# A decode kernel that streams K, V and weights: another window at the change of layers and another last step

## The chip, the cores and the metric

The kernel runs on one core of one Trainium2 chip. The metric is the device time of one execution in microseconds. The kernel before takes 2552.23 us, the median of three runs (2552.18 to 2552.38).

## The reference

Two requests (B = 2), one new token each, pass twice through the same block: attention over a cache, and then a mixer with a wide MLP. The residual stream is x, 2 x 576. Everything is bf16.

```
def _A_ref(x, k_cache, v_cache, wq, wo):          # 32 heads, 16384 cached rows of 128
    q = (x @ wq).reshape(B, Sq, H, Dh).transpose(0, 2, 1, 3)
    scores = einsum("bhqd,bhkd->bhqk", q, k_cache) * (Dh ** -0.5)
    p = _softmax(scores, axis=-1)
    o = einsum("bhqk,bhkd->bhqd", p, v_cache)
    return o.transpose(0, 2, 1, 3).reshape(B, Sq, H * Dh) @ wo

def _B_ref(x, w1, w2, w3, w4):
    h = _gelu(_layernorm(x, axis=-1) @ w1)
    hs = (the four quarters of h, each shifted along the sequence) @ w2
    x1 = x + hs
    return x1 + _gelu(_layernorm(x1, axis=-1) @ w3) @ w4

x = A_x
x = x + _A_ref(_layernorm(x, axis=-1), A_k_cache, A_v_cache, A_wq, A_wo)
x = x + _B_ref(_layernorm(x, axis=-1), B_w1, B_w2, B_w3, B_w4)
x = x + _A_ref(_layernorm(x, axis=-1), A_k_cache, A_v_cache, A_wq, A_wo)
x = x + _B_ref(_layernorm(x, axis=-1), B_w1, B_w2, B_w3, B_w4)
```

wq is 576 x 4096, wo 4096 x 576, w3 576 x 4608 and w4 4608 x 576. The sequence is one token long, so every shift moves in zeros: the mixer's `hs` is the same in both layers and doesn't depend on x. The caches are the same in both layers too, so what stays in the chip's memory over the change of layers is not read a second time.

## The kernel before, in words

**Tiles and memory.** A pair of request and head has one K tile and one V tile, each 128 partitions x 32,768 bytes (4 MB). There are 64 such pairs, called heads 0 to 63 below. One buffer `mem` holds everything that is read: 6,144 bytes a partition at its start (`AUX`, three chunks of transposed K, `kt`) and six slots of 32,768 bytes. `Store` (L269) gives the places out.

**One queue.** All reads are planned ahead in one list (`plan_all`, L509), and go out in that order, from one queue, SP's, by one helper line (L98). A piece is issued when its place is free, that is, when the last instruction that reads what stands there has run (`release`, L322, then `pump`, L290). A later piece never overtakes an earlier one. No planner sets the order of the compute instructions; it is written out in `layer`, `attention` and `last_head`.

**A layer.** `input_norm`, then q = xn @ wq (`cols_projection`, L821; wq lies in five pieces by rows, the fifth being half as high and folded, L845), then the heads. In each head half of K is transposed on TensorE, eight blocks of 128 columns at a time, into one of four PSUM buffers `tps` (`transposed`, L1176, one "chunk"), copied back to SBUF by ScalarE (L1200), and multiplied with q on TensorE (`scores`, L1210). The other half is multiplied with q on VectorE (`dots`, L1240, L1244). Softmax follows, and P.V on TensorE (`pv`, L1300). The middle heads run in a loop of the program (`loop`). `last_head` (L1082) writes out the last head together with the start of the next projection: `shares`, `normed` and `dealt` bring the heads' outputs into the form that wo needs, and `heads_projection` (L914) runs wo piece by piece. Then `two_norms`, w3 (`cols_projection`), a gelu (`gelu_z`), and w4 (`groups_projection`, L977, with `rows_step`, L900, L908). A group of w4 is n rows of 128 in one read; `GROUPS` lists the n.

**The change of layers.** Layer 1 begins with the heads whose tiles are still there: it takes the heads in the order 63, 61, 62, 0, 1 and so on (`order`, L560). K of 61, 62, 63 and V of 62 and 63 stay (`held`, L569), in slots 1 to 5. The weights between the two layers (wo, w3, w4 of layer 0 and wq of layer 1) pass through what is left, slot 0 and `AUX`: 38,912 bytes a partition. The pieces' places are written out in `plan_all`, each over the place of an earlier one. Behind wq the list goes on with V of head 61 (slot 0, in four parts), K of head 0 (slot 1), K of head 1 in two halves (slot 3), V of head 0 (slot 4), K of head 2 (slot 5, where K of 62 was), V of head 1 (slot 0), and from there K and V in turn.

In the gaps of that stretch, chunks of K 63 are transposed ahead of time (`ahead`, L673) and copied back by ScalarE to where they came from (`lay`, L690), so that layer 1's first scores need matmuls alone (`early_scores`). The last `LEAD` = 2 chunks stay in two of the PSUM buffers until layer 1 starts (`held_over`).

**The end.** w4 of layer 1 is added into `mps` as five column tiles of 128 (the fifth begins at column 448 and overlaps the fourth). `add_rows` (L970) adds it to x in two instructions, one for the four whole tiles and one for the fifth; `finish` (L1309) transposes the five tiles back to two rows (L1316), copies them to SBUF (L1319) and writes 2 rows of 1152 bytes.

## Time and profile before

| | |
|---|---|
| median of the runs | 2552.23 us |
| the profiled execution | 2552.28 us |
| its span | 2550.6 us |
| granted TensorE clock, mean | 0.653 |
| read from HBM | 1094.21 MB, 429 GB/s over the span |
| busy: PE, VectorE (DVE), ScalarE (ACT), GpSimd (POOL) | 60%, 74%, 44%, 6% |

The span begins and ends inside the execution: 1.7 us lie outside it (2552.28 - 2550.6). The page cuts the span into 40 slices of 63.8 us; layer 0's last tile lands in the 20th, and the weights of the change of layers are read in the 20th and 21st. In a timeline row the first number is the start in us from the start of the span, the second its length; rows of the same line that follow one another are drawn together with their count, and brackets at the end name how long the engine had been idle and what it waited for. "SPq" are the issues of reads. In a row of windows come the bounds, the length, then the busy time of PE, PE's weight loads, DVE, ACT and POOL with the count of instructions, the granted clock, the busy share of the 16 DMA engines, and what they moved in GB/s. In a row of groups by line come the line, the engine, the operation, the tiles, their shapes and the count, then the busy time in us and the mean of one in ns, then the idle time ahead of them. A row of DMA issues gives the count, the size of one and the median time from issue to landing.

### The profile page before, as it was taken

To read this page: it belongs to the slowest core of one execution; us is meant where nothing else is said; L and a number is where in the kernel's file an instruction comes from. 1 tells how busy PE (TensorE), PEld (TensorE's weight loads), DVE (VectorE), ACT (ScalarE), POOL (GpSimd) and SP (SyncE) were. 2 spreads that over 40 slices of the span, in tenths; PEclk is the share of its full clock that TensorE was granted. 3 is DMA by queue.
4 is the path that set the end of the run, shared out by engine and by line. 5 is a ranking of instruction groups with operands and counts; after the bars stand their busy time and mean duration, and the time that the engine had idled before them with its cause. 6 is when DMAs were issued, how large, how long until landed. Compare 5 with 4: busy or idle time off the path is not lost.

```text
span 2550.6 us, 75213 instructions
## 1 busy us (share of the span) xinstructions
PE 1522.6 (60%) x34456; PEld 1432.9 (56%) x34456; DVE 1888.3 (74%) x1924; ACT 1113.7 (44%) x1831; POOL 162.1 (6%) x151
## 2 busy tenths in 40 slices
...
DMA  9999999999999999999999999999999999999999
GB/s 412 428 434 430 433 431 433 430 433 431 433 431 433 430 433 430 433 430 434 425 417 431 431 434 430 433 430 433 430 433 430 434 430 433 431 433 431 433 431 376
DMA packets 44900, 1094.77 MB, mean 429 GB/s; under 512 B 4922, under 2 KB 6334, under 8 KB 9662
## 3 DMA queue, kind: packets, MB, share of 16 engines
...
HBM read 1094.21 MB, written 0.00 MB: 429 GB/s over the span
## 4 chain that ended last, share of the span: by engine, by line
DMA 71%; DVE 19%; issue 8%; PE 1%; SPq 0%; POOLq 0%; DVEq 0%; ACT 0%
DMA mem<-in_A_k_cache_dram 64%; DVE s_dve L1244 9%; DVE prod L1240 9%; DMA mem<-in_A_wo_dram 3%; DMA mem<-in_B_w_dram 2%; DMA mem<-in_A_v_cache_dram 2%; DMA mem<-in_A_wq_dram 0%; DVE mx L1249 0%; PE tps L1184 0%; DVE diag L1138 0%; DVE mx L1257 0%; SPq L98 0%; DVE q_col L1129 0%; DVE o_acc L1281 0%; DVE mx L1255 0%
## 5 line engine op out<-in xcount | busy, mean ns | idle before, releaser
L1200 ACT ACTIVATE mem<-tps 128x1024 bf16<-128x1024 bf16 x1018 | 955.7, 1036 | 1290.0 <-PE tps L1184 1287.5
L1184 PE MATMUL tps<-ident,mem 128*128 128x128 bf16 x8256 | 823.3, 271 | 707.8 <-POOLq L187 707.2
L1244 DVE TENSOR_REDUCE s_dve<-prod 128x16 f32<-128x2048 bf16 x508 | 1161.3, 2286 | 17.4
L1184 PEld LDWEIGHTS tps<-ident,mem 128*128 128x128 bf16 x8256 | 677.6, 124 | 717.7 <-POOLq L187 716.8
L1240 DVE TENSOR_TENSOR prod<-mem,qb 128x2048 bf16<-128x2048 bf16 x508 | 620.6, 1222 | 527.4 <-POOLq L187 518.9
L1300 PE MATMUL mps<-p,mem 128*128 128x1 bf16 x16384 | 450.7, 165 | 85.3 <-POOLq L187 78.2
L1300 PEld LDWEIGHTS mps<-p,mem 128*128 128x128 bf16 x16384 | 443.3, 103 | 100.2 <-ACT p L1274 97.0
L1210 PE MATMUL sps<-q_col,mem 128*128 128x1 bf16 x8144 | 368.7, 167 | 159.2 <-ACT mem L1200 142.9
L1210 PEld LDWEIGHTS sps<-q_col,mem 128*128 128x128 bf16 x8144 | 320.3, 101 | 217.4 <-ACT mem L1200 212.7
L1260 POOL PARTITION_ALL_REDUCE mx<-mx x128 | 160.2, 1252 | 2331.1 <-DVE mx L1257 2331.1
L1270 ACT ACTIVATE p<-s_dve,mx 128x64 bf16<-128x64 f32 x128 | 44.5, 348 | 15.5
L1148 ACT ACTIVATE qb<-sps 128x128 bf16<-128x128 f32 x129 | 34.0, 263 | 33.5 <-PE sps L1145 33.5
L1145 PE MATMUL sps<-diag,ones_bf 128*128 128x128 bf16 x129 | 29.8, 231 | 21.6 <-DVE diag L1138 21.6
L1274 ACT ACTIVATE p<-sps,mx 128x64 bf16<-128x64 f32 x128 | 37.5, 293 | 0.0
L1268 ACT ACTIVATE mx<-mx 128x1 f32<-128x1 f32 x128 | 30.6, 239 | 14.4 <-POOL mx L1260 14.4
L1138 DVE TENSOR_SCALAR diag<-ident,q_f 128x128 bf16<-128x128 bf16 x129 | 31.6, 245 | 0.0
L1249 DVE TENSOR_REDUCE mx<-s_dve 128x1 f32<-128x64 f32 x128 | 28.2, 220 | 4.5
L835 PE MATMUL sps<-xn,mem 128*128 128x2 bf16 x544 | 21.8, 175 | 12.3 <-DMA mem<-in_A_wq_dram 6.2
L835 PEld LDWEIGHTS sps<-xn,mem 128*128 128x128 bf16 x544 | 20.7, 122 | 13.5 <-DMA mem<-in_A_wq_dram 6.8
L1255 DVE TENSOR_REDUCE mx<-sps 128x1 f32<-128x64 f32 x128 | 27.4, 214 | 0.7 <-DVEq L259 0.7
L1145 PEld LDWEIGHTS sps<-diag,ones_bf 128*128 128x128 bf16 x129 | 12.6, 97 | 22.6 <-DVE diag L1138 22.6
L1274 ACT ACTIVATION_READ_ACCUMULATOR p<-sps,mx (+1 forms) x128 | 24.2, 189 | 0.0
...
## 6 DMA issues: line engine op xcount, KB each, us to landing
mem<-in_A_v_cache_dram SPq DMA_DIRECT2D x125, 4096.0 KB, 45.5
mem<-in_A_k_cache_dram SPq DMA_DIRECT2D x124, 4096.0 KB, 43.1
...
mem<-in_A_wq_dram SPq DMA_DIRECT2D x8, 1024.0 KB, 12.5
...
```

The lines of the kernel that those rows point to most:

```text
L835: ins = pe.matmul(out[:, m * B:(m + 1) * B], lhsT=buf[:, c:c + 127 * d + 1:d], rhs=self.xn[:, k, :], start=first and m == lo, stop=False, ...
L1145: self.pe(lambda pe: pe.matmul(qps, lhsT=self.ones_bf[:, :], rhs=self.diag[:, :], start=True, stop=True, skip_group_check=True), reads=["o ...
L1148: self.act(lambda e: e.activation(out=self.qb[s % self.NS][:, :], in_=qps, func=ACT.Copy), reads=[("qps", i)], writes=[("qb", s % self.NS) ...
L1184: ins = pe.transpose(self.tps[t][:, j * 128:(j + 1) * 128], buf[:, j * 128:(j + 1) * 128], self.ident[:, :])
L1200: self.act(lambda e: e.activation(out=self.kt[k], in_=self.tps[t][:, :].rearrange("p (i c) -> p i c", i=self.CH), func=ACT.Copy), reads=[( ...
L1210: ins = pe.matmul(self.sps[sp][:, c * self.CH + j:c * self.CH + j + 1], lhsT=self.kt[k][:, j, :], rhs=self.q_col[:, sp:sp + 1], start=True ...
L1240: self.dv(lambda e: e.tensor_tensor(out=prod, in0=buf.rearrange("p (j d) -> p j d", d=128), in1=qbc, op=ALU.mult), reads=[("qb", s % self. ...
L1244: self.dv(lambda e: e.tensor_reduce(out=sd[:, c0:c0 + DB], in_=prod, axis=AX.X, op=ALU.add), reads=["prod"], writes=[("s_dve", s % self.NS ...
L1260: self.pool(lambda e: e.partition_all_reduce(self.mx[:, 3, m:m + 1], self.mx[:, 2, m:m + 1], channels=128, reduce_op=ROP.max), reads=[("mx ...
L1270: self.act(lambda e: e.activation(out=p[:, n:self.NB], in_=self.s_dve[s % self.NS][:, :], func=ACT.Exp, bias=self.mx[:, 4, m:m + 1], scale ...
L1274: self.act(lambda e: e.activation(out=p[:, 0:n], in_=self.sps[i][:, 0:n], func=ACT.Exp, bias=self.mx[:, 4, m:m + 1], scale=self.scale, acc ...
L1300: ins = pe.matmul(self.mps[:, 448:449], lhsT=buf[:, j * 128:(j + 1) * 128], rhs=p[:, col:col + 1], start=(h == 0 and b == 0), stop=(h == 1 ...
```

## The change

**What stays.** The lower half of V of head 61 (`PART`, 16,384 bytes a partition in slot 0) also stays over the change of layers; the upper half is read again in two pieces of 8,192 bytes (`REST`). `partly`, `rename` and a new count in `used` do that: places are now released in steps of 16 blocks (`UNIT`) and not by halves of a tile or whole parts.

**Where the weights pass.** The first two chunks of K 63, and not the last two, stay in two PSUM buffers, and they are put there first, at the end of layer 0's heads; the early transposes pass through the two other buffers. The place of these two chunks in slot 1 (4,096 bytes a partition) becomes part of the window. The window is then the upper half of slot 0, these 4,096 bytes and `AUX`: bytes 22,528 to 43,007 and 0 to 6,143 of `mem`, 26,624 bytes a partition. `WINDOW` lists the places of the pieces: wo in 8 pieces (before 5), w3 in 9 (7), w4 in 9 (8, by the first tuple of `GROUPS`), wq in 6 (5). K of head 0 and K of the head after it are read in four quarters each (before in one piece and in two halves).

**Order.** `last_head` calls `keep_o` ahead of `shares`, and runs the half-groups of wo in front of `normed`; `ahead` and `lay` are called at other places and other counts.

**The end.** The last layer's w4 is computed in six column tiles of 96 (`EC`); each w4 group has 128 bytes (`CELL`) of room behind it, since the last tile's weight load reads 128 columns. x is cut anew into six tiles by GpSimd copies ahead of that (`recut`), one addition takes the place of two, one transpose the place of five, and the output is written as 12 rows of 192 bytes. w1's last read is in one piece and not two.

```diff
+    def rename(self, name, new, size):
+        at, _ = self.where.pop(name)
+        for c in self.cells(at, size):
+            assert self.owner[c] == name
+            self.owner[c] = new
+        assert name not in self.owner
+        self.where[new] = at, size
...
+    UNIT = 16
     WO_CUT = 5
     PK = ["prod", "gT", "hf", "every", "y0", "y"]
-    GROUPS = (6, 6, 6, 6, 6, 3, 2, 1)
+    GROUPS = ((4, 4, 5, 5, 5, 5, 5, 2, 1), (6, 6, 6, 6, 6, 3, 2, 1))
+    WINDOW = {
+        "wo": [38400, 1536, 22528, 33792, 29184, 38400, 0, 22528],
+        "w3": [(0, 0, 33792), (0, 1, 29184), (1, 0, 24576), (1, 1, 38400), (2, 0, 1536), (2, 1, 33792), (4, None, 29184), (3, 0, 38400), (3, 1, 0)],
+        "w4": [33792, 29184, 384, 23424, 37248, 31488, 384, 37248, 39552],
+        "wq": [(1, None, 22528), (2, None, 33792), (4, None, 0), (3, None, 22528), (0, 0, 38912), (0, 1, 2048)],
+    }
+    PART = 16384
+    REST = [(24576, 8192), (16384, 8192)]
     HEAD = (200, 60)
+    EC = 96
...
         self.early = ([(h, b, 2 * pb + h * (bp - pb) + b - pb) for h in range(2) for b in range(pb, bp, ch)] +
-                      [(h, b, h * pb + b) for h in range(2) for b in range(0, pb, ch)][:-self.LEAD])
+                      [(h, b, h * pb + b) for h in range(2) for b in range(0, pb, ch)][self.LEAD:])
...
-    def plan_tile(self, T, t, u, slot, parts=1, order=None):
+    def plan_tile(self, T, t, u, slot, cuts=None):
         b, hh = u % self.B, u // self.B
         src = T[b, hh].rearrange("(p j) d -> p (j d)", p=128)
-        if parts == 1:
+        if cuts is None:
...
+        self.parts[t, u] = self.slot(slot), [lo for lo, n in cuts] + [0] * ((t, u) == self.partly())
+        for lo, n in cuts:
+            self.store.plan((t, u, lo), f"part{slot}_{lo // 4096}", self.slot(slot) + lo, n,
+                            [(lambda m: m, src[:, lo // 2:(lo + n) // 2])])
+
+    def partly(self):
+
+        return "v", self.U - self.CARRY - 1
...
-    def plan_heads(self, l, ats):
+    def plan_heads(self, l, ats, parts=1):
 
         D, hg = self.D, self.HG
-        cuts = [(i, 0, hg) for i in range(self.ng - 1)] + [(self.ng - 1, 0, self.WO_CUT), (self.ng - 1, self.WO_CUT, hg)]
+        n = hg // parts
+        cuts = [(i, j, j + n) for i in range(self.ng - 1) for j in range(0, hg, n)]
+        cuts += [(self.ng - 1, 0, self.WO_CUT), (self.ng - 1, self.WO_CUT, hg)]
...
-        for i, (n, at) in enumerate(zip(self.GROUPS, ats)):
+        for i, (n, at) in enumerate(zip(self.GROUPS[l], ats)):
             self.cuts["w4", l].append((a, a + n))
-            self.store.plan(("w4", l, i), f"w4{i}", at, 2 * n * D, [
-                (lambda m: m, self.w4[a * 128:(a + n) * 128, :].rearrange("(p j) n -> p (j n)", j=n))])
+            self.store.plan(("w4", l, i), f"w4{i}", at, 2 * n * D + gap, [
+                (lambda m, n=n: m[:, 0:n * D], self.w4[a * 128:(a + n) * 128, :].rearrange("(p j) n -> p (j n)", j=n))])
...
+        r8 = row * self.HG
         assert r8 == w3r
-        self.plan_heads(0, [a, a + r8, a + 2 * r8, 0, a + 3 * r8])
-        self.plan_cols("w3", 0, self.w3, [(0, 0, mt // 2, a), (0, mt // 2, mt, a + w3r // 2),
...
-        b = a + w3r // 2
...
-        self.plan_groups(0, [b, b + g[0], b + 2 * g[0], b + 3 * g[0], 0, g[4], b, b + g[6]])
...
-        assert e + 3 * wqr <= s[1] and wqr // 2 + wqr <= e
+
+        def halves(n, pieces):
+            return [(k, (h or 0) * n // 2, n if h != 0 else n // 2, at) for k, h, at in pieces]
+        w = self.WINDOW
+        self.plan_heads(0, w["wo"], 2)
+        self.plan_cols("w3", 0, self.w3, halves(mt, w["w3"]))
+        self.plan_groups(0, w["w4"])
+        self.plan_cols("wq", 1, self.wq, halves(hd, w["wq"]))
...
-            self.plan_tile(source[t], t, u, ring[i], (4, 1, 2)[i] if i < 3 else 1, None if i else [1, 2, 3, 0])
+            q = self.TILE // 4
+            cuts = (self.REST, [(q * j, q) for j in (1, 3, 0, 2)], [(q * j, q) for j in (0, 2, 1, 3)])[i] if i < 3 else None
+            self.plan_tile(source[t], t, u, ring[i], cuts)
...
-        self.plan_small("w1", 1, self.w1, a, (0, 56, 64))
+        self.plan_small("w1", 1, self.w1, a, (0, 64))
...
-            if self.made == len(self.early):
-                if len(self.held_over) < self.LEAD:
-                    c = 2 * self.PB // self.CH - self.LEAD + len(self.held_over)
-                    self.transposes(1, 0, self.order(1)[0], c)
...
-            h, b, col = self.early[self.made]
-            self.made += 1
-            self.laid.append((h * self.BP + b, self.chunk % self.NT))
-            self.transposed(self.order(1)[0], h * self.BP + b)
+            u = self.order(1)[0]
+            c = len(self.held_over)
+            if c < self.LEAD:
+                at = self.chunk + len(self.early) + c
+                self.held_over.append((0, u, c, at))
+                self.transposed(u, c * self.CH, ("t", c), at % self.NT)
+                self.used(1, "k", u, c * self.CH, self.CH)
+            elif self.made < len(self.early):
+                h, b, col = self.early[self.made]
+                t = self.made % (self.NT - self.LEAD)
+                assert all(x != t for _, x in self.laid)
+                self.made += 1
+                self.laid.append((h * self.BP + b, t))
+                self.transposed(u, h * self.BP + b, None, t)
...
+        self.ahead(1 - l, 1)
...
-        self.ahead(l, 3)
+        self.ahead(l, 2)
...
-        self.lay(l, 4)
+        self.lay(l, 3)
...
+        if l == self.NL - 1:
+            self.recut()
+
+    def recut(self):
...
+        at = [(t, p) for t in range(KT) for p in range(0 if t < KT - 1 else TL, 128, 32)]
...
+            self.pool(lambda e, t=t, p=p, j=j, q=q, n=n: e.tensor_copy(out=self.x6[q:q + 32 * n, j, :],
+                                                                      in_=self.x[p:p + 32 * n, t, :]),
+                      reads=["x"], writes=["x6"])
+            g += n
...
-                        at = [self.block_cols(w, m + h * n // 2) for h in range(2)]
+                        at = [self.block_cols(w, m + h * n // 2, l) for h in range(2)]
...
                         for i, (c, d) in enumerate(at[:1] if at[0] == at[1] else at):
...
+    def rows_step(self, buf, a, b, ps, rhs, rk, pk, nm, first, m=128):
...
+        cols = self.kcol if m == 128 else range(0, D, m)
...
-                    o = (k - a) * D + self.kcol[t]
+                for t, c in enumerate(cols):
+                    o = (k - a) * D + c
...
             self.rows_step(self.store.buf(nm), a, b, self.mps, lambda k: self.gT[:, k * self.B:(k + 1) * self.B],
-                           "gT", "mps", nm, i == 0)
-            if i < 3:
+                           "gT", "mps", nm, i == 0, 128 if l < self.NL - 1 else self.EC)
+            if i < 3 or i == 4:
                 self.ahead(l, 1)
-            if i < 4:
+            if i < 6:
                 self.lay(l, 1)
             if i == 1:
                 self.side_norm(l)
             if i == 2 and l == self.NL - 1:
                 self.h_projection()
-        last = l == self.NL - 1
-        self.add_rows(self.xo[:, :, :] if last else self.x, "xo" if last else "x", self.mps, "mps")
+        if l < self.NL - 1:
+            self.add_rows(self.x, "x", self.mps, "mps")
+            return
+        m = self.EC
+        self.tt(self.xo[0:m, :, :].rearrange("p b t -> p t b"), self.x6[0:m, :, :],
+                self.mps[0:m, 0:self.ET * self.B].rearrange("p (t b) -> p t b", b=self.B), ALU.add,
+                ["x6", "mps"], ["xo"])
...
-        self.ahead(l, 1)
+        self.lay(l, 1)
+        self.ahead(l, 2)
         self.softmax_exp(s)
         self.touch(ACT.Sqrt)
         self.lay(l, 2)
         self.landed("v", u, False)
         for g in range(4):
             self.pv(l, s, u, g)
+        self.keep_o(s, None)
+        n = [sum(c[0] < a for c in self.cuts["wo", l]) for a in (1, 2)] + [len(self.cuts["wo", l])]
+        for i in range(n[0]):
+            self.heads_projection(l, i)
         self.shares(first, U)
-        self.keep_o(s, None)
-        self.heads_projection(l, 0)
         self.normed(l, first, U)
+        for i in range(n[0], n[1]):
+            self.heads_projection(l, i)
         self.dealt(late, U, self.sps[0], ("sps", 0), self.masked[1], self.oB[:, :], "oB")
-        self.heads_projection(l, 1)
         self.ahead(l, 1)
         self.lay(l, 1)
-        for i in range(2, len(self.cuts["wo", l])):
+        for i in range(n[1], n[2]):
             self.heads_projection(l, i)
...
-        parts = 2 if whole else self.parts[t, u]
-        size = self.NB // parts
-        part = b0 // size
-        self.uses[t, u, part] = self.uses.get((t, u, part), 0) + n
-        if self.uses[t, u, part] == size:
+        size = self.UNIT
+        for part in range(b0 // size, (b0 + n - 1) // size + 1):
+            k = min(b0 + n, (part + 1) * size) - max(b0, part * size)
+            self.uses[t, u, part] = self.uses.get((t, u, part), 0) + k
+            if self.uses[t, u, part] < size:
+                continue
             del self.uses[t, u, part]
+            lo, step = part * size * 256, size * 256
             if whole:
-                self.store.release((t, u), part * self.TILE // 2, (part + 1) * self.TILE // 2)
+                if l == 0 and (t, u) == self.partly() and lo < self.PART:
+                    continue
+                self.store.release((t, u), lo, lo + step)
             else:
-                self.store.release((t, u, part))
-
-    def transposed(self, u, b0, sig=None):
+                at = max(x for x in self.parts[t, u][1] if x <= lo)
+                self.store.release((t, u, at), lo - at, lo - at + step)
+        if l == 0 and whole and (t, u) == self.partly() and b0 + n == self.NB:
+            self.store.rename((t, u), (t, u, 0), self.PART)
...
+    def transposed(self, u, b0, sig=None, t=None):
...
-        self.chunk += sig is None
+        t = self.chunk % self.NT if t is None else t
...
-        def f(pe):
-            for t in [KT - 1] + list(range(KT - 1)):
-                c = self.kcol[t]
-                ins = pe.transpose(mb[0:B, c:c + 128], self.xo[:, t, :], self.ident[:, :])
-            return ins
-        self.pe(f, reads=["xo", "ident"], writes=["mps"])
-        self.dv(lambda e: e.tensor_copy(out=self.rows[0:B, 0:D], in_=mb[0:B, 0:D]), reads=["mps"], writes=["prod"])
-        o = g.dma("out", [(self.out.rearrange("b s d -> (b s) d"), self.rows[0:B, 0:D])], reads=["prod"])
+        m, n = self.EC, self.ET * B
+        self.pe(lambda pe: pe.transpose(mb[0:n, 0:m], self.xo[0:m, :, :].rearrange("p b t -> p (b t)"),
+                                        self.ident[0:m, 0:m]), reads=["xo", "ident"], writes=["mps"])
+        rows = self.rows[0:n, 0:m]
+        self.dv(lambda e: e.tensor_copy(out=rows, in_=mb[0:n, 0:m]), reads=["mps"], writes=["prod"])
+        o = g.dma("out", [(self.out.rearrange("b s (t c) -> (b s t) c", c=m), rows)], reads=["prod"])
```

74 lines of the change are left out of this document (32 added, 42 removed).

## The prediction

> **What bounds the kernel now.** I read the page first (totals, slices, queues, chain), then the windows and the DMA view of the plateau and of the change of layers, and last the timeline of the change and of the end.
>
> ```profile
> span 2550.6 us, 75213 instructions
> ...
> PE 1522.6 (60%) x34456; PEld 1432.9 (56%) x34456; DVE 1888.3 (74%) x1924; ACT 1113.7 (44%) x1831; POOL 162.1 (6%) x151
> ...
> DMA  9999999999999999999999999999999999999999
> GB/s 412 428 434 430 433 431 433 430 433 431 433 431 433 430 433 430 433 430 434 425 417 431 431 434 430 433 430 433 430 433 430 434 430 433 431 433 431 433 431 376
> ...
> HBM read 1094.21 MB, written 0.00 MB: 429 GB/s over the span
> ```
>
> All 40 slices have the DMA engines at nine tenths or more, and no compute engine is busy for more than 74% of the span. The kernel is a read of 1094 MB; it is faster only if it reads less, or loses less where the rate drops: slices 19 and 20 (change of layers) and the last.
>
> ```profile
> 1262.00:1275.00 13.00, 10.23 (x308) 9.77 (x308) 1.34 (x7) 2.62 (x3) 0.00 (x0) 0.50 1.01 417
> 1275.00:1288.00 13.00, 11.25 (x200) 11.01 (x201) 2.98 (x24) 4.86 (x8) 0.00 (x0) 0.50 1.01 411
> 1288.00:1300.00 12.00, 9.46 (x212) 8.30 (x209) 1.85 (x12) 5.51 (x7) 0.00 (x0) 0.50 1.02 418
> 1300.00:1312.00 12.00, 8.56 (x185) 7.97 (x186) 1.89 (x13) 3.51 (x5) 0.00 (x0) 0.50 1.02 424
> ```
>
> The last two numbers of a row are DMA share and GB/s. During the change of layers the queue is never empty (share 1.0), although the rate is 411 to 424 and not the 430 to 434 of most slices. So today's window for the weights hides every chain of small operations, and what is lost there is the price of small rows:
>
> ```profile
> DMA packets 8900, 259.08 MB, mean 432 GB/s; under 512 B 992, under 2 KB 992, under 8 KB 992
> ...
> DMA packets 1582, 9.11 MB, mean 414 GB/s; under 512 B 176, under 2 KB 176, under 8 KB 1021
> ...
> q8 instruction: 3, 0.05, 0.9%
> ```
>
> The first row is 400 to 1000 us, the others 1262 to 1284. Two equations, time = bytes/rate + packets x c/16, give c = 11.4 ns a packet on each engine. The last row: three packets of instructions took 0.9% of 16 x 22 us, 1.06 us each, on one engine each.
>
> **Part 1, bytes.** Half of V tile 61 is not read again: 2.10 MB at 432 GB/s is -4.85 us, if the queue stays full (-5.0 at the 418 of this stretch).
>
> **Part 2, more pieces.** wo is read in 8 pieces instead of 5, w3 in 9 for 7, w4 in 9 for 8, wq in 6 for 5; the rest of V 61 in 2 for 4, the first K tile of layer 1 in 4 for 1, the second in 4 for 2. That is 12 more; a piece is 128 rows and 16 semaphore writes, so 12 x 144 / 16 x 11.4 ns = +1.2 us while the queue is full, and nothing where it waits for an issue anyway. With the gaps found below I take a third, +0.4 (0 to 1.2).
>
> **Part 3, the smaller window.** Before, weights pass through 38,912 B a partition, 4.98 MB or 11.9 us at 418 GB/s. After, 16,384 + 6,144 + 4,096 = 26,624 B: 3.41 MB, 8.2 us. A freed place costs a round trip (issue, first data, last of 16 semaphore writes), which a deep queue hides. Its price from the only tile that meets an idle queue:
>
> ```profile
> 0.79 0.39 SPq L98 DMA_DIRECT2D mem<-in_A_k_cache_dram  x1
> ...
> mem<-in_A_k_cache_dram SPq DMA_DIRECT2D x1, 4096.0 KB, 12.5
> ```
>
> 12.5 us less 4.194 MB / 432 GB/s = 9.7 leaves 2.8 us fixed. Lower bound: the 2.2 KB of output are issued at 2549.01 and the span ends at 2550.6, so 1.6. Upper: one instruction packet in the way, 2.8 + 1.06 = 3.9. I take 2.8, because it is a load, through all 16 engines, as the pieces are.
>
> The Trainium skill, "DMA: Bandwidth & Descriptors" (section "Anatomy of one DMA"), puts the fixed cost at about 2.0 us, fitted on the path through GpSimd; this trace's 2.8 is above it. With 2.0 the sum would be 2549.6 (rival a) instead of 2553.5.
>
> The other durations, from the timeline of the change (PE, DVE, SP):
>
> ```profile
> 1225.69 0.33 SPq L98 DMA_DIRECT2D mem<-in_A_v_cache_dram  x1
> ...
> mem<-in_A_v_cache_dram SPq DMA_DIRECT2D x1, 4096.0 KB, 36.9
> ```
> ```profile
> 1257.15 1.04 PE L932 MATMUL sps<-l,mean_f 128*128 128x48 f32 x4
> ...
> 1262.80 3.55 PE L1300 MATMUL mps<-p,mem 128*128 128x1 bf16 x128 [1.55 <-POOLq L187]
> ...
> 1267.07 1.21 PE L908 MATMUL sps<-oA,mem 128*128 128x2 bf16 x40
> ...
> 1268.31 22.54 SPq L98 DMA_DIRECT2D mem<-in_B_w_dram  x15
> ...
> 1274.01 0.56 PE L908 MATMUL sps<-oB,mem 128*128 128x2 bf16 x15
> ...
> 1275.76 2.74 PE L1184 MATMUL tps<-ident,mem 128*128 128x128 bf16 x24
> ...
> 1278.37 3.25 PE L835 MATMUL sps<-xn,mem 128*128 128x2 bf16 x72
> ...
> 1284.15 1.14 PE L845 MATMUL sps<-xt,mem 128*128 128x4 bf16 x24
> ...
> 1286.78 0.89 PE L835 MATMUL sps<-xn,mem 128*128 128x2 bf16 x18 [0.40 <-DMA mem<-in_B_w_dram]
> ...
> 1289.05 0.96 PE L908 MATMUL mps<-prod,mem 128*128 128x2 bf16 x30 [0.50 <-DVE prod L1000]
> ...
> 1299.12 0.65 PE L908 MATMUL mps<-prod,mem 128*128 128x2 bf16 x15 [0.18 <-DMA mem<-in_B_w_dram]
> ...
> 1302.61 0.99 PE L835 MATMUL sps<-xn,mem 128*128 128x2 bf16 x32
> ...
> 1310.55 1.02 PE L835 MATMUL sps<-xn,mem 128*128 128x2 bf16 x32 [1.83 <-DMA mem<-in_A_wq_dram]
> ...
> 1316.03 1.23 DVE L1240 TENSOR_TENSOR prod<-mem,qb 128x2048 bf16<-128x2048 bf16 x1 [1.47 <-PE sps L1210]
> ...
> 1330.84 1.22 DVE L1240 TENSOR_TENSOR prod<-mem,qb 128x2048 bf16<-128x2048 bf16 x1
> ...
> 1345.81 0.33 SPq L98 DMA_DIRECT2D mem<-in_A_k_cache_dram  x1
> ```
>
> I walk the ring with two rules. A piece lands bytes/418 GB/s after the one before it, but not before its issue + 2.8 + bytes/418; it is issued 0.1 us after the last matmul that reads what stood in its place, in order (above, matmuls that end at 1267.07 + 1.21 = 1268.28 and an issue at 1268.31). 4,608 B a partition take 1.41 us, 5,760 take 1.76, 8,192 take 2.5, 4,096 take 1.25. On the kernel before, these rules give the end of the wq matmuls at 1311.6, as the row has it (1310.55 + 1.02). V 63 lands at 1225.69 + 36.9 = 1262.6 in both. After the change:
>
> wo: the first piece waits for the two chunks of K 63 to pass to PSUM and for the PE operation that then runs, 1257.15 + 1.04, about 1258.3; the queue still holds V 63, so nothing is lost. Pieces land 1264.0 to 1269.7. The P.V product ends at 1266.3, and two half-heads (0.61 each) free a place at 1266.9; that piece lands at 1271.2, the last at 1274.0; matmuls end 1274.6, as before (1274.57). The fixed 2.8 first shows here, by 0.1.
>
> w3: two pieces are in flight; the third place is freed by the last of wo (1274.6), so it lands at 1278.9 instead of 1278.2. PE starts 3.6 us after wo (now 3.8: 1274.57 to 1278.37, three chunks of transposes of 0.91 stand before it, later two). A half-piece takes 0.9 (0.89 by its row); the fourth freed place is issued at 1279.1; the tail piece needs 36 matmuls for 24, as the halves of the uneven groups no longer pair (1.7 for the row's 1.14). w3 ends at 1288.4 (before 1287.7).
>
> w4: gelu 1.4 us; pieces land at 1289.0, 1290.8, 1293.1 (its place is freed at 1288.4), then 1.8 apart to 1300.2, 1301.0, 1301.4. End 1301.6 (before 1299.8).
>
> wq: the second piece waits for the last of w4, 1301.7, and lands at 1307.0; the fourth waits for the first, which PE starts 2.8 after w4; the halves land at 1312.1 and 1313.7. End 1314.2 (before 1311.6): +2.6.
>
> The gaps of these four stages add to 3.1 us. Of V 61 and the two K tiles nearly nothing waits. Then layer 1 computes two heads from tiles already there, bound by DVE, so K of head 2, the sixth of the order, issued at 1345.81 into the place of the second of those heads when that is done, now goes out at 1348.4. V of head 0, before it, has landed at 1348.9: a last gap of 2.3 us. K lands at 1361.2, against 1345.81 + 15.2 = 1361.0:
>
> ```profile
> mem<-in_A_k_cache_dram SPq DMA_DIRECT2D x1, 4096.0 KB, 15.2
> ```
>
> After that a head takes 14.8 us of DVE (1316.03 to 1330.84) and two tiles, 19.4 us, of DMA, so DMA is the bound again and everything shifts alike. So parts 1 and 3 together are 5.5 us of gaps against 5.0 saved, +0.5. To it I add instruction packets: about eight of 1.06 us fall between 1259 and 1312, a piece is there when the slowest engine has it, and a deep queue hides that where a shallow one does not: 0 to 8 us, I take 1.0, near the low end, as most fall on an engine that is ahead. The other new waits cost nothing here: with two PSUM buffers instead of four for the early transposes, a transpose waits for the ScalarE copy two back, 1.04 us each and done a stage earlier; if that cover goes, it is 1 us each on PE, four times at most.
>
> ```profile
> L1200 ACT ACTIVATE mem<-tps 128x1024 bf16<-128x1024 bf16 x1018 | 955.7, 1036 | 1290.0 <-PE tps L1184 1287.5
> ...
> L1316 PE MATMUL mps<-ident,xo 128*2 128x128 bf16 x5 | 0.7, 302 | 0.5 <-DVE xo L596 0.5
> ```
>
> (The groups by line; the second row is for the end.) SP's queue holds nothing but these loads, so behind a piece that waits stand only later pieces.
>
> **Part 4, the end.**
>
> ```profile
> 2546.70 0.66 PE L908 MATMUL mps<-prod,mem 128*128 128x2 bf16 x15 [0.17 <-DMA mem<-in_B_w_dram]
> 2547.39 0.36 DVE L596 TENSOR_TENSOR xo<-st,mps 128x8 bf16<-128x8 f32 x2 [3.00 <-PE mps L908]
> 2547.80 0.69 PE L1316 MATMUL mps<-ident,xo 128*2 128x128 bf16 x5 [0.45 <-DVE xo L596]
> 2548.54 0.45 DVE L1319 COPY prod<-mps 2x576 bf16<-2x576 bf16 x1 [0.79 <-PE mps L1316]
> 2549.01 0.27 SPq L98 DMA_DIRECT2D out_dram<-prod  x1
> ```
>
> After the last piece 18 matmuls for 15 (+0.13), one addition for two (-0.18), one transpose for five (0.30, row L1316, for 0.69: -0.39), a copy of 12 x 96 for 2 x 576 (0.22 for 0.45, an estimate: the additions of 8 columns take 0.18 each: -0.23): -0.65, between -1.0 and +0.5. The extra matmuls before and the GpSimd copies of x lie under the DMA, which PE waits for. The Trainium skill, same page, "Specifications", says that transfers under 512 B are read, modified and written; the output rows fall from 1152 to 192 B, and no run here prices that.
>
> **Sum.** 2552.28 (profiled run, 0.05 above the median 2552.23) + 0.5 + 0.4 + 1.0 - 0.65 = 2553.5 us.
>
> **The rivals.** (a) The window is deep enough: with the output's round trip of 1.6 the same walk ends wq at 1311.1. Then only K of head 2, still issued at 1345.8 because compute got no faster, leaves a gap, of 1.1; K and V land 3.9 us earlier; with part 2 in full and part 4, 2552.28 - 3.9 + 1.2 - 0.65 = 2548.9. A round trip 0.4 longer ends wq at 1311.3 and gives 2549.6, the other end of this case. For it: share 1.0 in every window now, and the output's 1.6. Against: 2.8 at the first tile. The Trainium skill's 2.0 (the section above) would be this case. (b) The other side, slower: the round trip is 3.5 to 3.9, since the slowest of 16 engines meets an instruction packet on most turns. At 3.5 the walk ends wq at 1318.4 and the V tile after K at +5.4, which with parts 2 and 4 is 2557.4; at 3.9, +8.4 and 2560.4. So 3.5 is where it passes 0.2%. For it: 1.06 us each, one every 7 us, against seven turns that depend on each other; against: now no wait shows them. (c) The tail does not get shorter, since small output rows cost what the copies save: +0.65 on any case.
>
> **How the numbers follow.** Forecast case 2550 to 2557: 0.52. (a) 0.24. (b) 0.24. Can't be told from no change within 0.2%, 5.1 us, 2547.1 to 2557.3. Even full hiding, with no gap at all, gives 2552.28 - 4.85 + 1.2 - 0.65 = 2548.0, so faster by more than 0.2% is 0.04; slower is nearly all of (b), 0.22; same 0.74. The range leaves out a tenth at each end: 2548.2 to 2560.
>
> **What would show it.** Right: bytes read 2.1 MB fewer; weights landing 4 to 6 us after issue instead of 7 to 11; DMA share under 1 in some windows from 1265 to 1350, most near 1348; wq ending near 1314; the last addition to the output's issue about 1.0 us instead of 1.6. Wrong: share 1.0 throughout and K of head 2 issued at 1345.8 (a); wq after 1318 (b).

## The result: slower by 9 us, and the profile after

The changed kernel takes 2561.33 us, the median of six runs (2560.58 to 2564.74); the kernel before takes 2552.20 beside it (2551.95 to 2552.38). The ratio is 1.0038, with a 95% interval of 1.0025 to 1.0051: +9.1 us, where 2553.5 was forecast. The profiled execution is the fastest of the six, 2560.58 us.

The page after, totals and slices:

```profile
span 2558.7 us, 75319 instructions
...
DMA  9999999999999999999999999999999999999999
GB/s 409 430 432 431 433 431 431 434 429 432 434 430 431 433 431 431 433 431 431 409 349 423 432 433 430 432 432 431 433 431 431 433 431 432 431 432 433 430 432 380
...
HBM read 1092.11 MB, written 0.00 MB: 427 GB/s over the span
```

The 2.10 MB are saved. The plateau is as before. The whole loss is in slices 20 to 22: 409, 349 and 423 GB/s, where before had 425, 417 and 431. The windows of that stretch (bounds, length, busy time of PE, weight loads, DVE, ACT and POOL with counts, granted clock, DMA share, GB/s), after:

```profile
1262.00:1275.00 13.00, 10.97 (x315) 10.24 (x313) 1.47 (x7) 3.98 (x5) 0.00 (x0) 0.50 0.99 384
1275.00:1288.00 13.00, 8.72 (x169) 8.11 (x170) 3.20 (x25) 3.72 (x6) 0.00 (x0) 0.50 0.96 355
1288.00:1300.00 12.00, 8.72 (x172) 7.65 (x170) 1.72 (x11) 5.85 (x8) 0.00 (x0) 0.50 0.95 349
1300.00:1312.00 12.00, 7.33 (x154) 6.29 (x152) 1.69 (x11) 4.53 (x6) 0.00 (x0) 0.50 0.86 322
1312.00:1324.00 12.00, 6.79 (x203) 6.38 (x201) 1.19 (x7) 2.75 (x5) 0.00 (x0) 0.50 0.95 333
```

Look at the last two numbers together. The share still says 0.95 while the rate is 349: a packet that is under way counts as busy however slowly it goes, so in this stretch only GB/s tells how much is lost. The trace keeps every packet, and a data packet here is one partition's row of a piece: of the 4,229 data rows that begin in 1262 to 1324, 164 took more than twice the median of their size (the longest 2.33 us, where the median is 0.31); before, it was 19 of 3,704. Over 1262 to 1324 after moved 21.53 MB and before 25.94; the 4.41 MB between them are 10.5 us at 418 GB/s. Two more views, the DMA issues of 1268.2 to 1291 us (count, size, median us from issue to landing) and the timeline of PE, show the same from the side of the pieces:

```profile
mem<-in_B_w_dram SPq DMA_DIRECT2D x11, 576.0 KB, 5.6
```
```profile
1273.45 1.44 PE L956 MATMUL sps<-oB,mem 128*128 128x2 bf16 x40 [1.17 <-DMA mem<-in_A_wo_dram]
...
1289.17 0.84 PE L882 MATMUL sps<-xn,mem 128*128 128x2 bf16 x18 [0.55 <-DMA mem<-in_B_w_dram]
...
1306.06 0.29 PE L956 MATMUL mps<-prod,mem 128*128 128x2 bf16 x5 [1.42 <-DMA mem<-in_B_w_dram]
...
1317.93 1.01 PE L882 MATMUL sps<-xn,mem 128*128 128x2 bf16 x32 [3.96 <-DMA mem<-in_A_wq_dram]
...
1320.45 0.58 PE L882 MATMUL sps<-xn,mem 128*128 128x2 bf16 x16 [0.70 <-DMA mem<-in_A_wq_dram]
```

The eleven pieces of 4,608 bytes a partition in that view (nine of w3, two of w4) land 5.6 us after their issue by the median; the forecast's price of a place is 2.8 + 1.41 = 4.2. PE ends wo at 1274.89, w3 at 1290.01, w4 at 1306.35 and wq at 1321.03 (start plus length of the rows), against 1274.6, 1288.4, 1301.6 and 1314.2 by the walk. The wait of 3.96 us is for a wq piece whose place came free late (issue at 1310.07), but not for that alone. A read is shared by the 16 DMA engines, and the trace has 16 landing signals for each: 15 parts of this piece were there by 1315.34, and the last at 1317.89.

K of head 2 then goes out, in the timeline of SP, and its DMA row gives the time to landing:

```profile
1355.35 0.33 SPq L98 DMA_DIRECT2D mem<-in_A_k_cache_dram  x1
...
mem<-in_A_k_cache_dram SPq DMA_DIRECT2D x1, 4096.0 KB, 15.7
```

The table follows the landings, after minus before:

| piece | before | after | shift | gap added here |
|---|---|---|---|---|
| end of w3 | 1286.74 | 1289.12 | +2.4 | 2.2 (V 63 was at +0.2) |
| end of w4 | 1299.43 | 1306.02 | +6.6 | 4.2 |
| end of wq | 1310.51 | 1320.40 | +9.9 | 3.3 |
| K of head 1 | 1341.39 | 1349.54 | +8.1 | 3.1 (with 4.85 saved at V 61) |
| K of head 2 | 1361.00 | 1371.07 | +10.1 | 1.9 |
| last weight piece | 2547.01 | 2555.85 | +8.8 | |
| output's issue | 2549.01 | 2557.07 | +8.1 | |

The gaps add to 14.7 us; the forecast had 5.5. About 1.0 us comes back between the last V tile (+9.8) and the last weight piece.

The end, in the timeline after:

```profile
2553.60 2.62 PE L956 MATMUL mps<-prod,mem 128*128 128x2 bf16 x72 [0.95 <-DMA mem<-in_B_w_dram]
2556.32 0.19 DVE L619 TENSOR_TENSOR xo<-x,mps 96x12 bf16<-96x12 f32 x1 [3.04 <-PE mps L956]
...
2556.57 0.24 PE L1375 MATMUL mps<-ident,xo 96*12 96x96 bf16 x1 [0.35 <-DVE xo L619]
2556.85 0.20 DVE L1378 COPY prod<-mps 12x96 bf16<-12x96 bf16 x1 [0.34 <-PE mps L1375]
2557.07 0.34 SPq L98 DMA_DIRECT2D out_dram<-prod  x1
```

From the end of the last matmul (2556.22) to the output's issue it is 0.85 us, before 1.65. This part does what it says.

### The profile page after: what moved, and what is told of

It reads as the page before. It is cut to its first block, busy times and chain, and to the rows that moved or that the text cites. A ratio compares the mean times of both kernels' runs of the same rounds, so it can differ in the third digit from the quotient of the medians.

```text
span 2558.7 us, 75319 instructions
## 1 busy us (share of the span) xinstructions
PE 1526.8 (60%) x34500; PEld 1438.4 (56%) x34500; DVE 1888.2 (74%) x1923; ACT 1114.5 (44%) x1831; POOL 164.4 (6%) x163
## 4 chain that ended last, share of the span: by engine, by line
DMA 70%; DVE 20%; issue 8%; PE 1%; SPq 1%; POOLq 0%; DVEq 0%; ACT 0%
DMA mem<-in_A_k_cache_dram 64%; DVE s_dve L1305 9%; DVE prod L1301 9%; DMA mem<-in_B_w_dram 3%; DMA mem<-in_A_wo_dram 2%; DMA mem<-in_A_v_cache_dram 1%; SPq L98 0%; DMA mem<-in_A_wq_dram 0%; DVE mx L1310 0%; DVE diag L1195 0%; DVE mx L1318 0%; DVE q_col L1186 0%; DVE o_acc L1342 0%; DVE mx L1316 0%; PE tps L1245 0%
## 5 line engine op out<-in xcount | busy, mean ns | idle before, releaser
L1342 DVE COPY o_acc<-mps 128x1 f32 (+1 forms) x130 | 19.3, 149 | 7.6 <-PE mps L1361 7.6
```

## The experiments

The theory behind the forecast: a freed place costs a constant round trip, and the window holds enough pieces to hide nearly all of it. The result is 9 us off that, so the runs ask three things: is it the window or another part of the change; does the round trip of a place stay constant; do instruction packets make it long (the reason that rival (b) gave)?

### One part alone: the end

`before` with the six tiles of 96, `recut` and the one transpose, and with nothing of the change of layers; and the same with w1's last read in one piece.

```diff
+    EC = 96
...
-        self.plan_groups(1, [b, s[1], ...])
+        self.plan_groups(1, [b, s[1], ...], CELL)
...
+        if l == self.NL - 1:
+            self.recut()
```


> The kernel before with the new end alone (six column tiles, one addition, one transpose, 12 rows of output). The prediction's sum for it is -0.65 us, 2551.55 against 2552.2; the trace of the changed kernel has 1.22 us from the last landing to the output's issue where the kernel before has 2.00, so -0.8, 2551.4. The rival that small output rows cost what the copies save: 2552.2.

```diff
-        self.plan_small("w1", 1, self.w1, a, (0, 56, 64))
+        self.plan_small("w1", 1, self.w1, a, (0, 64))
```


> As e1_tail, and w1's last read in one piece of 64 rows and not 56 + 8. The prediction gave that edit nothing: then 2551.4 as e1_tail. The trace of the changed kernel has w1 there 0.35 us before the last piece of wo, where before it came 1.24 us behind it; if that is worth something at the end, it is 0.65 us: 2550.8.

The end alone takes 2551.51 us (2551.29 to 2551.90) against 2552.24 beside it: -0.73; the ratio is 0.9997 (0.9988 to 1.0006), so the interval alone doesn't tell it from none, but the slowest of its 11 runs is only 0.04 above the fastest of the 33 of before (2551.86). With w1's cut it is 2551.78 (2551.66 to 2552.12), so that cut costs 0.27 and gains nothing. The forecast's -0.65 for the end holds, and the loss lies in the change of layers.

### The window, with everything else kept

The changed kernel with the whole of V 61 read again, so that the window is 43,008 bytes, and the same pieces at other places; 28 to 32 KB a partition of reads stand behind each piece as far as the end of w4, then 15 to 22 KB for wq.

```diff
-    PART = 16384
-    REST = [(24576, 8192), (16384, 8192)]
+    PART = 0
+    REST = [(8192, 8192), (16384, 8192), (24576, 8192), (0, 8192)]
...
-        "wo": [38400, 1536, 22528, 33792, 29184, 38400, 0, 22528],
+        "wo": [6144, 10752, 15360, 22528, 27136, 31744, 0, 38912],
```


> The changed kernel with all its small pieces, but V 61 is not kept: its lower half's place joins the window (43,008 bytes a partition), and each piece has its place where 28 to 32 KB were read behind the piece that stood there. V 61 is read whole again, 2.1 MB or 4.85 us more. Theory (small window, round trip longer than 2.8 us): no gaps, 2552.2 + 0.4 to 1.2 for pieces - 0.65 to 1.4 for the end = 2551 to 2553. Rival (the pieces and their packets cost it): the loss stays and the bytes come on top, 2561.3 + 4.9 = 2566; anything above 2558 speaks for it.

The second keeps a quarter of V 61, with a window of 34,816 bytes.

```diff
-    PART = 16384
+    PART = 8192
```


> As the changed kernel, but a quarter of V 61 is kept and not a half: window of 34,816 bytes a partition, 23 KB read behind most pieces before their place is needed (the changed kernel: 14 KB; at 418 GB/s 7.1 and 4.2 us). Theory (small window): a place is needed again later than a round trip of 4.1 us plus the piece's 1.4, so gaps only at wq (0 to 3 us): 2552.2 - 2.4 - 0.65 to 1.4 + 0.4 to 1.2 + 0 to 3 = 2548 to 2553. Rival (pieces): about 2563.7.

The first takes 2555.03 us (2554.09 to 2557.25; ratio 1.0013, interval 1.0004 to 1.0022), which is 6.3 us faster than the changed kernel although it reads 4.85 us more, and still 2 us above the 2551 to 2553 that were expected. Its windows (columns as above):

```profile
1275.00:1288.00 13.00, 9.51 (x193) 8.95 (x194) 3.28 (x25) 3.72 (x6) 0.00 (x0) 0.50 1.02 410
...
1300.00:1312.00 12.00, 7.93 (x169) 6.79 (x166) 1.70 (x11) 4.54 (x6) 0.00 (x0) 0.50 0.92 352
```

Up to the end of w4 it is late by 0.72 us, of which 0.22 is V 63: six more pieces cost 0.5, where the forecast's 144 / 16 x 11.4 ns a piece gives 0.6. So the new order, the two PSUM buffers and the many pieces cost next to nothing there. What it loses it loses behind w4, +1.55 at wq and +2.6 at V 61: at the very places where I had left only 15 to 22 KB. The changed kernel, with 9 to 18 KB, has 14.7 us of gaps to this one's 3.7 (K of head 2 lands 3.92 late, less 0.22). The smaller window is what costs the 11 us between them.

The quarter takes 2555.05 (2553.66 to 2557.09; ratio 1.0009, interval 1.0000 to 1.0018), also above what was expected (2548 to 2553). Its wq pieces had only 9 to 12 KB behind them, and its wq ends 4.98 us late.

### A round trip by itself

All layers are left out; what is computed is no longer the reference. 72 pieces of 4,608 bytes a partition (590 KB, 1.41 us at 418 GB/s) pass through n = 1 to 6 places, 12 for each n; 18 matmuls read a piece and free its place.

```diff
+        for depth in (1, 2, 3, 4, 5, 6):
+            for i in range(12):
+                nm = ("piece", depth, i)
+                a = (len(todo) % 7) * n // 2
+                self.store.plan(nm, f"piece{i % depth}", self.slot(0) + (i % depth) * n, n, [(lambda m: m, flat[:, a:a + n // 2])])
...
+        for nm in todo:
...
+                for c in range(18):
...
+            self.store.release(nm)
```


> The round trip by itself, with nothing else running: pieces of 128 x 4,608 bytes of K pass through 1, 2, 3, 4, 5 and then 6 places (12 pieces each), each piece read by 18 matmuls and its place given to the next. All layers are left out, so its output and its time are not the kernel's. If the fixed part of a round trip is the forecast's 2.8 us, one place gives a period of 0.1 + 2.8 + 1.4 + about 0.9 = 5.2 us, and four places keep the queue full (period 1.4). If it is the 4.1 us that makes the forecast's walk end where the changed kernel did, one place gives 6.5 us and four do not.

The windows of the ring, one stretch for each n from 1 to 6 (bounds, length, PE, weight loads, POOL, granted clock, DMA share, GB/s), and below them the DMA issues in the same stretches (count, size, median us from issue to landing):

```profile
9.00:53.00 44.00, 6.39 (x180) 5.58 (x180) 0.00 (x0) 1.00 0.45 134
60.00:87.00 27.00, 6.41 (x180) 5.59 (x180) 0.00 (x0) 1.00 0.73 218
92.00:111.00 19.00, 5.75 (x162) 5.01 (x162) 0.00 (x0) 1.00 0.84 281
115.00:133.00 18.00, 5.82 (x165) 5.02 (x162) 0.00 (x0) 1.00 0.98 334
137.00:152.00 15.00, 5.76 (x162) 5.02 (x162) 0.00 (x0) 1.00 1.00 373
162.00:173.00 11.00, 4.47 (x126) 3.90 (x126) 0.00 (x0) 1.00 1.02 402
```
```profile
mem<-in_A_k_cache_dram SPq DMA_DIRECT2D x10, 576.0 KB, 3.7
...
mem<-in_A_k_cache_dram SPq DMA_DIRECT2D x10, 576.0 KB, 4.8
...
mem<-in_A_k_cache_dram SPq DMA_DIRECT2D x9, 576.0 KB, 5.2
...
mem<-in_A_k_cache_dram SPq DMA_DIRECT2D x11, 576.0 KB, 6.0
...
mem<-in_A_k_cache_dram SPq DMA_DIRECT2D x8, 576.0 KB, 6.8
...
mem<-in_A_k_cache_dram SPq DMA_DIRECT2D x5, 576.0 KB, 7.8
```

One piece alone takes 3.7 us, which leaves 2.3 of fixed cost: less than the forecast's 2.8. But the time grows with the pieces in flight, and does so before the rate is full: by the forecast's rules one to four places give about 120, 240, 360 and the full 418 GB/s, and these windows have 134, 218, 281 and 334. Five and six places, 23 and 28 KB a partition, give 373 and 402. The share reads 0.98 at 334 GB/s, much as in the changed kernel. A window also holds the pieces with which one depth passes into the next, and instruction packets; for four places and more that makes it low, as the next run shows.

The Trainium skill, "DMA: Bandwidth & Descriptors" (section "Anatomy of one DMA"), has about 2.0 us that scale with nothing, for a DMA issued from GpSimd (these are issued from SP). For one piece alone the 2.3 here is near it; two in flight take 4.8 us, 3.4 past a piece's own bytes, so no one constant describes a place.

### The same with fewer instructions, and in other cuts

Two matmuls instead of 18 for a piece, so that the whole run reads one instruction packet and not ten, and none in the stretches below (and PE is 0.5 us quicker with a piece); layers left out as above.

```diff
-                for c in range(18):
+                for c in (0, 17):
```


> The ring of e5 (1 to 6 places of 4,608 bytes, 12 pieces each, layers left out), but 2 matmuls read a piece and not 18, so that there is hardly an instruction packet (one for e5's nine). Theory that these packets make the stalls of e5's rings of 3 to 6 places: with F = 2.3 a piece takes 2.3 + 1.4 + 0.2 = 3.9 us round, so three places already run at a period of 1.4 us without a stall. Rival (a piece that reaches the engines when they are about to run dry starts anew, whatever the packets): two places keep e5's period of 2.75 and not 1.95, and three still stall.

The windows for n = 2, 3 and 4:

```profile
52.00:75.00 23.00, 2.13 (x20) 1.31 (x20) 0.00 (x0) 1.00 0.82 253
80.00:98.00 18.00, 1.91 (x18) 1.18 (x18) 0.00 (x0) 1.00 0.91 303
103.00:118.00 15.00, 1.92 (x18) 1.18 (x18) 0.00 (x0) 1.00 0.99 365
```

For one to six places it is 151, 253, 303, 365, 402 and 411 GB/s. With two, a piece comes every 2.33 us (0.590 MB / 253 GB/s), where the 2.3 of a lone piece would give 1.95, and three do not fill the engines either: there, instruction packets are not the reason. Four is another matter. Landing by landing, the pieces of this run with four places in use come 1.46 us apart from 109.79 to 120.00, which is 404 GB/s; the next comes 2.48 us later, and the run's one packet of 16 KB begins at 119.15. In the first ring they come 1.39 to 1.42 us apart from 121.06 to 135.84, but for one gap of 3.55, beside a packet at 127.14. So four places run nearly full where no packet meets them, and a packet of 0.9 to 1.0 us on one engine comes with a loss of 1.1 and of 2.1 us.

What two and three places lack is to be seen in the landing signals and the rows of this run, counted for each n from its n-th landing to its last:

| places | issue to first of 16 parts, median us | first to last part, median us | rows over twice the median (0.18 us) | GB/s |
|---|---|---|---|---|
| 1 | 3.2 | 0.5 | 180 of 1408 | 148 |
| 2 | 3.3 | 1.2 | 148 of 1292 | 247 |
| 3 | 3.4 | 1.7 | 71 of 1087 | 326 |
| 4 | 4.2 | 2.1 | 25 of 1039 | 372 |
| 5 | 5.2 | 1.6 | 7 of 761 | 417 |
| 6 | 6.1 | 2.2 | 0 of 606 | 416 |

With one to three places the first part lands 3.2 to 3.4 us after the issue: the start gets hardly dearer. It is the last part, the one that frees the place, that falls further behind. Of a lone piece the first 16 rows, which begin 0.95 to 1.60 us after its issue, take up to 1.04 us, and nearly all later ones about 0.18; with one and two places there are about 16 slow rows for each piece (180 for 11 pieces, 148 for 10), with five and six hardly any. The reading that fits is that an engine which has run dry begins anew with a slow row, and that a piece waits for the slowest of 16. Which engine moved a row is not in the trace, and why such a row is slow stays open.

Then 18,432 bytes as 2, 4 and 8 pieces, and 27,648 bytes as 3, 6 and 12.

```diff
+        for k, (n, depth, pieces) in enumerate([(9216, 2, 12), (4608, 4, 24), (2304, 8, 48), (9216, 3, 12), (4608, 6, 24), (2304, 12, 48)]):
```


> The same 18,432 bytes of places cut as 2 x 9,216, 4 x 4,608 and 8 x 2,304, then 27,648 bytes as 3, 6 and 12 (layers left out; every 128 x 128 block read by one matmul). If the bytes in flight alone count, the rate is one and the same for a size of the ring: about 320 GB/s for the first three (e5 with four places: 316) and about 400 for the others. If a finer cut helps, since a place is given back sooner, 8 places are nearer to full rate than 2; with 2 places of 9,216 the formula 2.3 + 2.8 + 1.3 = 6.4 us for 2 pieces gives 369 GB/s.

The windows in that order:

```profile
5.00:40.00 35.00, 11.95 (x389) 11.16 (x390) 0.00 (x0) 1.00 0.94 350
45.00:78.00 33.00, 13.12 (x373) 11.40 (x370) 0.00 (x0) 1.00 0.99 367
84.00:116.00 32.00, 16.23 (x369) 12.87 (x366) 0.00 (x0) 1.00 1.04 389
122.00:150.00 28.00, 10.30 (x332) 9.57 (x333) 0.00 (x0) 1.00 1.00 409
...
190.00:222.00 32.00, 17.07 (x393) 13.63 (x390) 0.00 (x0) 1.00 1.06 391
```

It is mostly the bytes in flight that count: 18 KB a partition give 350 to 389, 27 KB give 391 to 411. Finer pieces help a little where bytes are few (350 to 389), and cost where they are enough (409 to 391). With eight places of 2,304 bytes the pieces come 0.75 us apart nearly throughout, where 418 GB/s would be 0.71: that ring hardly runs dry, and what it lacks is the price of shorter rows.

### Finer pieces in the kernel

If that holds in the kernel, finer cuts of wo, w3, w4 and wq through the same 26,624 bytes should gain. Two forms; the first lays two pieces into the first 6,144 bytes of `mem`.

```diff
-    GROUPS = ((4, 4, 5, 5, 5, 5, 5, 2, 1), (6, 6, 6, 6, 6, 3, 2, 1))
+    GROUPS = ((2, 2, 2, 3) * 3 + (3, 2, 2, 2), (6, 6, 6, 6, 6, 3, 2, 1))
...
-        self.plan_heads(0, w["wo"], 2)
+        self.plan_heads(0, w["wo"], 4)
```


> The changed kernel with the same window (half of V 61 kept) and its weights cut about half as large (wo 14 pieces, w3 17, w4 16, wq 9): about 18 KB are then read behind a piece before its place is needed, where the changed kernel has 9 to 18. If the ring's table holds in the kernel (18,432 bytes as 4 pieces 371 GB/s, as 8 pieces 389; 13,824 bytes as 3 places 293), w3, w4 and wq go from the 322 to 355 GB/s of the changed kernel's windows to 370 to 390: 15.3 MB, 44 us before and 39 to 41 after, so -3 to -5 us, 2556.5 to 2558. If more pieces only cost packets (24 more, 2.5 us by the 11.4 ns of the prediction): 2564.

> e11 cut its weights finer and lost 16 us, but its trace shows matmuls of wo that waited 6.6 us for the landing of a w3 piece beside theirs: two pieces shared a 2,048-byte unit of the first 6,144 bytes, by which the kernel keeps its waits. Here one piece at a time stands there, and 13 to 18 KB are read behind a piece (changed kernel: 9 to 18). By the ring (8 pieces of 2,304: 389 GB/s, 4 of 4,608: 352 to 371, 3: 293): -2 to -4 us, 2557 to 2559.5. If finer pieces only cost packets: 2563 or more.

The first takes 2577.71 us (2577.27 to 2578.44), 16 more than the changed kernel, and by a fault of its own, which the timeline of PE shows:

```profile
1279.43 1.23 PE L956 MATMUL sps<-oA,mem 128*128 128x2 bf16 x40 [6.57 <-DMA mem<-in_B_w_dram]
```

A wo matmul waits 6.57 us for a w3 piece: the program keeps waits by cells of 2,048 bytes, the two pieces (2,304 bytes each) share one, and so the earlier one's reader waits for the later one too. It says nothing of the theory. The second form has no shared cell and takes 2564.52 (2564.05 to 2566.24; ratio 1.0049, 1.0035 to 1.0062): 3 us more than the changed kernel, where 2 to 4 less were expected. The number is that of the expectation's other case (finer pieces only cost packets, 2563 or more), but the windows do not show a full queue with dearer rows. With 13 to 18 KB behind a piece of wo and w3 (in the changed kernel 9 to 18) this stretch ran slower than there (332 GB/s for 355), and in 1262 to 1324 there are 226 slow rows for 164:

```profile
1275.00:1288.00 13.00, 7.07 (x148) 6.06 (x144) 3.27 (x25) 3.72 (x6) 0.00 (x0) 0.50 0.94 332
```

The expectation of a gain falls. Why finer pieces help in the ring and not here stays open.

### A quarter, with deeper places for wq

The quarter again, with wq in halves and places with 15 to 32 KB behind each.

```diff
-        "wq": [(1, None, 34816), (2, None, 21376), (4, None, 30592), (3, None, 34816), (0, 0, 0), (0, 1, 14336)],
+        "wq": [(1, 0, 512), (1, 1, 26624), (2, 0, 30720), (2, 1, 34816), (4, None, 38912), (3, 0, 14336), (3, 1, 18432), (0, 0, 512), (0, 1, 22528)],
```


> e4 (a quarter kept, 34,816 bytes) with wq in halves and places such that 15 to 32 KB are read behind every piece, where e4 had 9 to 12 at wq. Theory: no gap up to V 61; then K of head 2 is issued at about 1345.9 as in the kernel before, since compute sets it, so that of the 2.4 us of bytes only what is left at its landing counts (e8: 0.3 of 1.2): 2552.25 - 0.75 for the end - 0.3 + 0.5 to 1.2 for pieces = 2551.5 to 2552.5. Rival (the bytes come through in full): 2550.

It takes 2553.69 us (2552.99 to 2554.96), 1.4 less than the first quarter, at 1.0006 of before (0.9997 to 1.0015). The end of wq is 2.87 us late and not 4.98 (the first quarter's profile is of its slowest run, so about 2 us of its lateness are that run's). Placing alone moves the time, but a window of 34,816 bytes still costs more than the quarter saves: with the shorter end in it the kernel stands 1.5 us above before (2552.20), which the interval does not tell from none, and above the 2551.5 to 2552.5 that were expected.

### Instruction packets

896 one-column memsets on GpSimd in the middle of `last_head`, in the kernel before and in the changed one: they work on a tile of their own, and only make GpSimd read more instructions.

```diff
+        if l == 0:
+            def f(e):
+                for c in range(32):
+                    ins = e.memset(self.idle[:, c:c + 1], 0)
+                return ins
+            for _ in range(28):
+                self.pool(f, writes=["idle"])
```


> The kernel before, and 896 tiny GpSimd instructions (writes of one byte a partition to a place nobody reads) behind the landing of V 63, which bring 3 to 4 more instruction packets of 16 KB into the change of layers. No gaps there, so every theory expects 0 to +1 us (the packets' bytes are 0.15 us; one engine falls 1 us behind at a time).

> The same 896 GpSimd instructions in the changed kernel. Theory that instruction packets set what a round trip takes above 2.8 us (the queue runs dry, all engines wait for the one that was late): 3 to 4 packets x up to 1 us, +2 to +4 us, 2563 to 2565. Rival (the round trip is longer by itself): 0 to +1, 2561 to 2562.

Both came out against the theory. The changed kernel takes 2561.21 us (2560.86 to 2562.17), as without them, where 2 to 4 us more were expected. The packets that came were seven of 8 KB and 0.3 to 0.5 us, though, not the 3 to 4 of 16 KB that the expectations speak of. The kernel before takes 2555.18 (2554.41 to 2556.16; ratio 1.0012, 1.0003 to 1.0021): +2.9, where a deep queue was to hide them. Its DMA view of 1262 to 1324 has seven packets more than before's one:

```profile
q14 instruction: 8, 0.07, 0.3%
```

They come about every 4.85 us, and the last of a piece's landings falls behind its first by steps of 0.65 to 0.75 us at that pace, to 5.65 us (before 2.9). The signals show how: of the fifth w4 piece 15 parts are there by 1297.29 and the last at 1300.26, where before has 1297.12 and 1297.29. So one of 16 parts falls behind by some 3 us, and while the queue is full it does not catch up. That it is the engine which carries these packets is argued from the pace and not shown. VectorE is slower beside the memsets too (4.53 us busy for 2.98 in 1275 to 1288), but compute is not what delays this stretch: 15 parts of the last w4 piece land only 0.16 us later than before. In the changed kernel with the packets the last part stays within 1.1 us of the fifteenth up to the end of wq; its queue runs dry between pieces, which would let such an engine catch up, and that is argued, too.

### The rule used for a better version

An eighth of V 61 is kept (4,096 bytes), in return for the 4,096 bytes of the two chunks in PSUM: the window stays at 38,912 bytes, with the kernel before's larger pieces. The order, the PSUM buffers and the end are those of the change.

```diff
-    GROUPS = ((4, 4, 5, 5, 5, 5, 5, 2, 1), (6, 6, 6, 6, 6, 3, 2, 1))
+    GROUPS = ((6, 6, 6, 6, 5, 4, 2, 1), (6, 6, 6, 6, 6, 3, 2, 1))
...
-    PART = 16384
-    REST = [(24576, 8192), (16384, 8192)]
+    PART = 4096
+    REST = [(12288, 8192), (20480, 8192), (28672, 4096), (4096, 8192)]
```


> The changed kernel with an eighth of V 61 kept (4,096 bytes a partition) and not a half: the two chunks of K 63 in PSUM give back just what the eighth takes, so the window is 38,912 bytes as before, and the pieces are those of before (one w4 group apart). Theory (the loss is all in the small window): no gaps, 2552.24 - 1.05 MB / 432 GB/s (2.4... a quarter would be; the eighth is 0.52 MB, 1.2 us) - 0.7 for the end = 2550.3, within 0.5. Rival (something else in the change costs: the two PSUM buffers, the order in the last head): 2551.5 or more.

It takes 2551.23 us (2550.71 to 2552.29) against 2552.26 beside it: -1.03, where -1.9 was expected; ratio 0.9997, interval 0.9988 to 1.0006. It is the fastest kernel of the study, by a difference that the interval does not tell from none. Its windows are full again, and K of head 2 goes out where it did before:

```profile
1275.00:1288.00 13.00, 10.75 (x200) 10.32 (x201) 3.23 (x25) 3.95 (x7) 0.00 (x0) 0.50 1.01 409
...
1300.00:1312.00 12.00, 7.92 (x173) 6.92 (x174) 1.74 (x13) 4.54 (x6) 0.00 (x0) 0.50 1.02 420
```
```profile
1345.91 0.33 SPq L98 DMA_DIRECT2D mem<-in_A_k_cache_dram  x1
...
mem<-in_A_k_cache_dram SPq DMA_DIRECT2D x1, 4096.0 KB, 14.8
```

w4 lands at -0.03 and wq at +0.12 to before, so the two PSUM buffers and the new order cost nothing. V 61 lands 0.99 early, V of head 0 still 0.68, K of head 2 only 0.32: it is issued at 1345.91 (before 1345.81), when the compute of the first heads has freed its place, and no byte saved ahead of it brings that forward. Nearly all of the gain is the end's.

## Why the prediction was wrong

**Part 1, bytes: right in size, without effect.** 2.10 MB less are read, and V 61 alone recovers 4.85 us of the shift. But K of head 2 waits for compute, and compute for wq: wq ends 9.46 us late (1321.03 for 1311.57), K goes out 9.54 late (1355.35 for 1345.81) and lands 10.1 late. The saved bytes stand between the two and are used up by the wait. The forecast had this step ("now goes out at 1348.4", a last gap of 2.3), and the eighth of V 61 shows the same on an undisturbed window.

**Part 2, more pieces: right.** 0.5 us for six more pieces with a full queue; 0.4 was taken for twelve with gaps.

**Part 3, the smaller window: the step that failed is "I take 2.8", one fixed price for every freed place.** By it four pieces of 4,608 bytes fill the queue, and the gaps come to 5.5 us. Measured are 14.7. The start of a piece is not dearer than forecast (a lone piece takes 2.3 past its bytes), but a place comes free only when the last of 16 parts is in, and with two and three pieces in flight this comes 1.2 to 1.8 us behind the first, where a lone piece has 0.5. So two and three places gave 218 and 281 GB/s in the ring, where 2.8 gives about 240 and 360. The changed kernel, which leaves 9 to 18 KB behind a piece, so two to four pieces, ran at 322 to 384. There, too, the first part landed as early as in the ring where the queue had run short (3.24 us after the issue at 1267.09, 3.07 at 1274.91, 3.24 at 1287.97), and three pieces waited 1.1, 1.5 and 2.6 us for their last part alone: the first of w3, the last of w4 and the fourth of wq. The slow rows of 1262 to 1324 go with the loss from kernel to kernel: 16 (the eighth), 38 (V 61 read again), 79 and 109 (the quarters), 164 (the change) and 226 (the fine cut), with wq's last landing 0.1, 1.6, 2.9, 5.0, 9.9 and 13.2 us later than before, which has 19.

The size of this term accounts for nearly all of the miss. The gaps of 14.7 us stand against 5.5 for the window, 0.4 for pieces and 1.0 for packets, and 1.0 came back: 14.7 - 5.5 - 0.4 - 1.0 - 1.0 = 6.8, against 2560.58 - 2553.5 = 7.1 in the profiled run.

The price was read from the first tile, 4 MB that go into idle engines. It could not show how pieces behave one after another, and the two bounds set for it, 1.6 and 3.9, were both from single transfers.

A second sentence failed with it: "Of V 61 and the two K tiles nearly nothing waits". They waited 3.1 us. w3 and w4 hold 6.4 of the gaps, wq 3.3, and V of head 0 with K of head 2 1.9, where 2.3 was forecast for the last.

**Instruction packets: whether the term of 1.0 us is right stays open.** Seven more in the changed kernel moved nothing, but they were small ones, and the term is about those of 16 KB and 1.06 us. Two of these came with 1.1 and 2.1 us in rings of four places, and in the changed kernel one begins at 1274.77, beside the first piece of w3, whose last part is 1.1 us late. What the seven of 1262 to 1324 cost together no run separates. Rival (b) had the price right (3.9 gives 2560.4; 2560.58 was profiled) and its reason in part: a piece is there when the slowest engine has it, as the signals show. But it wanted a packet on most turns, and the ring without any in its stretches still falls short with two and three places; nor does one run beside the late last parts of w4 (slow rows from 1304.02 on) and of wq's fourth piece (a row of 2.33 us from 1313.08 on). That the number fits so well is luck.

**PSUM, order, SP: right.** The transposes on two buffers cost nothing (w4 -0.03, wq +0.12 with the window of before).

**Part 4, the end: right.** -0.73 alone for -0.65. Rival (c) falls: the span ends 1.6 us after the output's issue in both (2558.7 - 2557.07, and before's 2550.6 - 2549.01). The Trainium skill, "DMA: Bandwidth & Descriptors" (section "Specifications"), has transfers under 512 B read, modified and written; by these 1.6 us that shows no price with 12 rows of 192 B here.

**What was to be seen.** Right: bytes, the pieces of w3 landing 4 to 6 us after their issue (5.6), the last addition to the output's issue short (0.75 us, 2556.32 to 2557.07). Wrong: the larger pieces of w4 and those of wq, which landed after 6.4 to 7.4 us by their medians; wq's end, 1321.03 for 1314 and past the 1318 that was to speak for rival (b); and the place of the gaps: the lowest window is 1300 to 1312, not near 1348.

**Open:** why an engine that has run dry takes up to 1 us in the ring and 2.3 in the kernel over a row of 0.18 or 0.31; how much of the gaps is from instruction packets of 16 KB; why about 1.0 us comes back in layer 1; why finer pieces do not help in the kernel.
